# Routing attention followed by a mixture of experts: key masks on GpSimd, a first pair in halves, and three moved steps

## The chip, the cores and the metric

The kernel runs on one core of a Trainium2 chip. The metric is the device time of one execution in microseconds (us). A core has five engines that each work through a queue of their own, in order: TensorE multiplies matrices (its weight loads are shown apart), VectorE and ScalarE work on tensors element by element, GpSimd does so too and issues the indirect transfers, and SyncE issues most of the other transfers. Semaphores join them.

## The reference

Four batches, eight heads, 768 tokens, 64 values per head, and 16 cluster centroids per head. A query sees a key only where both have the same nearest centroid. The attention's output, 3072 rows of 512, then goes through a mixture of eight experts, of which each row takes one.

```
# q, k, v: 4 x 8 x 768 x 64; centroids: 8 x 16 x 64
q_assign = argmax(einsum("bhsd,hcd->bhsc", q_n, c_n), -1)   # q_n, k_n, c_n: normalised
k_assign = argmax(einsum("bhsd,hcd->bhsc", k_n, c_n), -1)
mask = q_assign[:, :, :, None] == k_assign[:, :, None, :]
attn = softmax(where(mask, q @ k.T / sqrt(64), -1e9))       # denominator + 1e-9
x = (attn @ v), laid out as 3072 x 512
logits = x @ w_gate                                         # 8 experts
e = argmax(logits); gate = softmax(logits)[e]
y = gate * (relu(x @ w1[e]) @ w2[e])                        # w1: 8 x 512 x 1024, w2: 8 x 1024 x 512
```

## The kernel before

*Attention.* The work is cut into 16 pairs: one batch and two heads, which share the 128 partitions (64 values each). Each pair goes through two halves of its 384 queries (`HS`) and six blocks of 128 keys. A slot is one block of one half, slots 0 to 11. In a slot `score` (L384) emits two f32 matmuls K x Q into a PSUM bank pair `sps` (three of them), two bf16 matmuls of 32 rows of a key mask and a query mask on top of that (`score_half`, L373 to L382, the matmuls at L379), and an exponential on ScalarE (L392) that writes one of twelve tiles `A`. The key mask `mk` and the query mask `mq` come from the one-hot cluster numbers, the key mask scaled by 2^60 and shifted, so that the exponential of a pair of different clusters is zero. `add_up` (L394) adds the tiles up on VectorE, one addition per slot from block 1 on. When all twelve slots are through, `attend` (L400) multiplies the tiles with V, half by half, and ScalarE copies each result to `oT`; slot 12 is between the two halves, slot 13 behind them. `sum_up` (L416) sums the accumulated tiles over the partitions on TensorE, in slot 2 of the next pair, and computes the pair's share of the gate's logits; `weights_of` (L433) takes the reciprocals, `rows` and `store` (slot 4) bring the output to DRAM.

*Preparing a pair.* `prepare(n, step)` (L469) has six steps. Step 0, `turn` (L274), is two VectorE transposes of q and k. Step 1, `similar` (L308), is four matmuls with the centroids. Step 2 (`assign0`, `assign1`, L322 to L334) and step 3 (`assign2`, L336) are seven VectorE instructions from the similarities to the transposed one-hots `ohT` (L348). Step 4, `place(n, 1)`, writes the key mask with four VectorE instructions (L361), and step 5, `place(n, 0)`, the query mask with four ScalarE copies (L359). Step 0 of pair n + 2 stands behind slot 12 of pair n (L837); steps 1 to 5 of pair n + 1 stand in slots 2, 5, 7, 8 and 11 of pair n (in pair 0, step 1 in slot 4), at L779.

*The first pair.* Its q and k come as two transfers each (L184), one of SyncE and one of ScalarE, in pieces of 256 bytes; twelve TensorE transposes (L267) and four copies (`first_turn`, L279) turn them, and the five steps for pair 0 follow one after the other (L819). The values of pair 0, the loads of pair 1 and the centroids' way to DRAM and back are issued in between.

*Gating.* While pairs 4 to 6, 8 to 10 and 12 to 13 run, the rows of the batch before are gated: `gate`, `gate_sum`, `choose`, `count` and `number` (L542), whose last act is six indirect transfers of GpSimd (L554) that scatter each row's record to its expert's list. `number` stands in slot 6 of pairs 6 and 10 and slot 3 of pair 13.

*Mixture of experts.* Ten turns, each one expert with a fixed number of rows (288, 288, 256, 288, 288, 384, 416, 416, 448, 128). `gather` (L685) fetches rows with indirect transfers, `weigh` (L702) scales them, `turn_rows` (L727) transposes them. `layer1` (L895) computes relu(x w1) with Strassen's scheme in Winograd's form: seven products instead of eight (L916), from sums of rows (`x_sums`), sums of weights (`w1_sums`, L756; all sums at L736) and additions of results (`add`, L874). It goes through two column halves; each half has seven places called hooks, 0 to 6 and 7 to 13, where other work may be put. In a half the hooks 4 and 5 of the seven come right behind the two additions. `h_sums` (L973) and `layer2` (L999) do the same for the second layer, with hooks of their own, and `write` (L991) scatters the rows. The dictionaries `h1` and `h2` say what stands at which hook of layers 1 and 2. The next turn's weight sums are given by `when` (L1158 to L1163); in turn 1 the sums 2 and 1 stand at hooks 9 and 10 of layer 1. In turn 3, `ask` (L622, hook 5) tests on VectorE that all softmax sums lie in a safe range, and `answer` (L632, hook 9) adds up the verdicts; a program that finds them outside runs a slower path at the end.

*The order of work.* Each engine's queue is the order in which the code emits instructions; nothing reorders them. The tile library adds the semaphores. So the hooks and slots decide what stands in front of what.

```
            for u, step in ((2 if n else 4, 1), (5, 2), (7, 3), (8, 4), (11, 5)):
                at_pair(n, u, prepare, n + 1, step)
...
            at_pair(n + 2 - last, 3 if last else 6, number, b)
...
                elif s == 1:
                    when = ((h1, 9), (h1, 10), (h2, 2), (h2, 3), (h2, 6), (h2, 6))
```

## Time and profile before

| | |
|---|---|
| median of three runs | 671.11 us (671.42, 668.75, 671.11) |
| the profiled execution | 672.25 us, of which the span of the profile is 670.7 |
| mean granted clock of TensorE | 0.992 |
| ScalarE | 300.0 us busy, 45% of the span |
| additions of `A` on VectorE, L398 | 160 of them, 0.945 to 0.948 us each |
| exponentials, L392 | 192, 0.811 us each |
| score matmuls, L379, f32 | 768, 159.3 us busy |
| first product of the experts' turns (L916) | starts at 337.1 us of the span |

The profile is one execution. Its first part gives each engine's busy time and share of the span; the second cuts the span into forty slices of 16.8 us, with a digit for the tenths of a slice in which an engine was busy. Groups of instructions are named by line, engine and operation, with the output on the left of the arrow. A row of a timeline shows the start, the duration of a run of like instructions, and in brackets the idle time ahead of them and what ended it. A row of TensorE's waits shows what waits, for what, and then the sum of the idle time, the number of waits and the longest. Durations of several instructions in one row run from the first's start to the last's end.

### The profile page before, as it was taken

Reading aid. Unit: us, or ns where it says so; the run is one execution under the profiler, and the core shown is the slowest. Engines: PE = TensorE matmul, PEld = TensorE weight load, DVE = VectorE, ACT = ScalarE, POOL = GpSimd, SP = SyncE. Lnnn points to the kernel's source line nnn. Section 1 sums busy time; section 2 is a strip of 40 time slices with the busy share of each in tenths; the row PEclk is TensorE's granted clock in tenths of the full one; section 3 lists DMA queues with packets and bytes.
Section 4 is the critical chain, followed back from the end, with each engine's and each line's share of the span. In section 5 each row is a group of like instructions: output and inputs, shape, how many; then the busy total and the mean of one; then the engine's idle time right before and its main releaser. Section 6 shows DMA issues by size and latency. Waiting matters only on the chain.

```text
span 670.7 us, 11366 instructions
## 1 busy us (share of the span) xinstructions
PE 649.9 (97%) x4210; PEld 425.7 (63%) x4210; DVE 512.3 (76%) x901; ACT 300.0 (45%) x522; POOL 127.3 (19%) x156
## 2 busy tenths in 40 slices
PE   5999999999999999999999999999999999999995
PEld 2444444454444455444575879989798887969773
DVE  5889999999999999999886868878778366572300
ACT  3666556657556565556622333243332331423210
POOL 4100000012000300033104704225240422130010
PEclk9899999999999999999999989999999999999998
DMA  6843455433455443347475586685675844625010
GB/s 118 191 86 72 82 95 95 66 73 72 77 95 95 65 81 73 70 115 239 115 266 142 189 297 217 253 321 156 275 239 229 261 160 138 221 93 182 8 48 18
DMA packets 191806, 95.36 MB, mean 142 GB/s; under 512 B 155967, under 2 KB 173887, under 8 KB 190464
## 3 DMA queue, kind: packets, MB, share of 16 engines
q1 hardware_dynamic: 184560, 81.15, 44.0%
q0 software_dynamic: 4928, 12.97, 5.8%
q8 instruction: 35, 0.57, 0.4%
q10 hardware_dynamic: 2256, 0.44, 0.4%
q14 instruction: 27, 0.22, 0.1%
HBM read 74.10 MB, written 20.70 MB: 141 GB/s over the span
## 4 chain that ended last, share of the span: by engine, by line
PE 77%; issue 9%; DVE 7%; POOL 2%; DMA 2%; ACT 1%; POOLq 0%; SPq 0%; DVEq 0%; ACTq 0%
PE sps L379 20%; PE mps L404 15%; PE bank L916 9%; PE sbank L916 7%; PE bank L1017 7%; PE bank L1036 7%; PE sbank L1017 5%; PE mps L427 2%; PE mps L312 2%; DMA xg<-x_rows,gi 1%; PE bank L885 1%; DVE acc L398 1%; DVE v L736 1%; DVE xT L727 1%; POOL tokens_of L554 1%
## 5 line engine op out<-in xcount | busy, mean ns | idle before, releaser
L392 ACT ACTIVATE A<-sps 128x768 f32<-128x768 f32 x192 | 153.5, 811 | 44.9 <-PE sps L379 44.1
L379 PE MATMUL sps<-qT,kT 64*128 64x384 f32 x768 | 159.3, 494 | 0.6 <-ACT A L392 0.6
L398 DVE TENSOR_TENSOR acc<-acc,A 128x768 f32<-128x768 f32 x128 | 121.4, 948 | 10.1 <-ACT A L392 2.8
L404 PE MATMUL mps<-A,v_in 128*64 128x384 f32 x768 | 127.4, 488 | 0.0
L379 PEld LDWEIGHTS sps<-qT,kT 64*128 64x128 f32 x768 | 67.1, 188 | 55.0 <-issue 51.4
L404 PEld LDWEIGHTS mps<-A,v_in 128*64 128x64 f32 x768 | 53.8, 137 | 70.5 <-issue 61.7
L991 POOL DMA_INDIRECT out_dram<-z,si x30 | 47.6, 1587 | 198.4 <-DVE z L874 169.3
L554 POOL DMA_INDIRECT tokens_of<-tg,pos_i x24 | 26.7, 1111 | 281.9 <-DVE pos_i L552 148.2
L379 PE MATMUL sps<-mq,mk 64*128 64x384 bf16 x384 | 63.5, 325 | 2.6 <-DVE mk L361 2.6
L1036 PE MATMUL bank<-w,h 128*128 128x512 f32 (+2 forms) x224 | 64.4, 596 | 0.0
L685 POOL DMA_INDIRECT xg<-x_rows,gi x30 | 42.7, 1423 | 48.2 <-DVE si L676 18.1
L359 ACT COPY mq<-ohT 32x384 bf16<-32x384 bf16 x62 | 31.6, 510 | 42.7 <-DVE ohT L348 41.8
L916 PE MATMUL sbank<-xc,a 128*128 128x144 f32 (+4 forms) x288 | 48.0, 310 | 0.2
L916 PE MATMUL bank<-xT,w 128*128 128x144 f32 (+4 forms) x288 | 47.8, 309 | 0.0
L874 DVE TENSOR_TENSOR h<-sbank,p 128x288 f32<-128x288 f32 (+4 forms) x18 | 9.2, 512 | 48.3 <-PE sbank L916 48.3
L916 PEld LDWEIGHTS bank<-xT,w 128*128 128x128 f32 x288 | 43.8, 191 | 2.6 <-issue 2.2
L1036 PEld LDWEIGHTS bank<-w,h 128*128 128x128 f32 (+2 forms) x224 | 24.7, 152 | 32.5 <-issue 32.3
L916 PEld LDWEIGHTS sbank<-xc,a 128*128 128x128 f32 x288 | 43.3, 191 | 0.9 <-ACT sbank L940 0.6
L379 PEld LDWEIGHTS <-mk 64*128 64x128 bf16 x384 | 19.5, 95 | 28.0 <-DVE mk L361 3.4
L934 ACT ACTIVATE h<-h 128x288 f32<-128x288 f32 (+4 forms) x36 | 17.6, 488 | 42.7 <-DVE h L874 42.5
L702 DVE TENSOR_TENSOR xw<-xg,sf 128x256 f32<-128x256 f32 (+2 forms) x60 | 32.8, 606 | 1.8 <-DMA xg<-x_rows,gi 1.6
L398 DVE TENSOR_TENSOR acc<-A 128x768 f32<-128x768 f32 x32 | 30.2, 945 | 3.1 <-ACT A L392 2.9
(208 smaller groups left out, 890.7 us busy)
## 6 DMA issues: line engine op xcount, KB each, us to landing
w<-in_moe_w_dram SPq DMA_DIRECT2D x20, 2048.0 KB, 12.0
v_in<-in_v_dram SPq DMA_DIRECT2D x32, 192.0 KB, 2.8
x_rows<-x SPq DMA_DIRECT2D x64, 96.0 KB, 2.4
turn_rows<-xw SPq DMA_DIRECT2D x23, 256.0 KB, 2.0
q_in<-in_q_dram SPq DMA_DIRECT2D x60, 96.0 KB, 3.2
k_in<-in_k_dram SPq DMA_DIRECT2D x60, 96.0 KB, 3.2
xs<-turn_rows SPq DMA_DIRECT2D x16, 144.0 KB, 2.8
xs<-turn_rows SPq DMA_DIRECT2D x8, 208.0 KB, 4.2
```

The source lines that it names most:

```text
L359: (nc.gpsimd.tensor_copy if n == 0 and h else nc.scalar.copy)(dst, src)
L379: nc.tensor.matmul(SP[n, h, j][:, a, 0:HS], lhsT=kt[rows, j * P : (j + 1) * P], rhs=qt[rows, h * HS : (h + 1) * HS], start=first, stop=not ...
L392: nc.scalar.activation(A[n, h, j], ps[:, :, 0:HS], AF.Exp, scale=D**-0.5)
L398: nc.vector.tensor_tensor(ACC[n, h], first, A[n, h, j], op=ALU.add)
L404: nc.tensor.matmul(O[n, h][D * a : D * (a + 1), 0:HS], lhsT=VIN[n][:, a, j, :], rhs=A[n, h, j][:, a, :], start=(j == 0), stop=(j == NQ - 1),)
L554: ins = nc.gpsimd.indirect_dma_start(out=t_d[:, :], out_offset=bass.IndirectOffsetOnAxis(ap=pos_i[:, i : i + 1], axis=0), in_=tg[:, b, i, ...
L685: nc.gpsimd.indirect_dma_start(out=xg[0:m], out_offset=None, in_=x_d[0:rows_in, :], in_offset=bass.IndirectOffsetOnAxis(ap=g["gi"][0:m, j ...
L702: nc.vector.tensor_tensor(xw[0:m, :, :, d2 * a : d2 * (a + 1)], xg[0:m].rearrange("p (r a d b) -> p a r b d", r=HP, a=2, b=DB)[:, a], g["s ...
L916: nc.tensor.matmul(ps[:, f * T2 : (f + 1) * T2], lhsT=w[:, k, (2 * j + f) * P : (2 * j + f + 1) * P], rhs=x[:, k, :], start=first and f + ...
L991: ins = nc.gpsimd.indirect_dma_start(out=out[:, :], out_offset=bass.IndirectOffsetOnAxis(ap=GR[s]["si"][0:rows, j : j + 1], axis=0), in_=z ...
L1017: nc.tensor.matmul(ps[:, 0:H], lhsT=x[:, k, :], rhs=y[:, k, :], start=first and k == 0, stop=k == 3, skip_group_check=not first,)
L1036: nc.tensor.matmul(ps[i * m : (i + 1) * m, :], lhsT=h[:, f, j * P : j * P + m], rhs=w[:, f, :], start=(k == 0), stop=(k == FB // n - 1),)
```

## The change

The change has six parts.

1. Pair 0. q and k come in one transfer each, both on SyncE, in pieces of 1536 bytes; the values of pair 0 and the loads of pair 1 stand right behind them, and the gate's weights move from ScalarE's queue to SyncE's. A new function `start_first` takes the place of the transposes, of `first_turn` and of the five steps: q and k are turned by matmuls with the identity, half by half, and copied by ScalarE; the similarities, the seven VectorE steps and the masks are done for each half of queries and keys, and the scores of blocks 0 to 2 stand in between. `assign0` to `assign2` get a `part` argument for that. The centroids' transfer to DRAM comes last.
2. The key masks of pairs 1 to 15 are written by GpSimd instead of VectorE. In pair 0 they stay with VectorE, while six of the eight query mask copies go to GpSimd.
3. In pair 0 the steps 1 to 4 for pair 1 stand in slots 6, 7, 8 and 9.
4. Step 0 of pair n + 2 stands in slot 10 of pair n instead of behind slot 12: ahead of the addition of the pair's last block.
5. In turn 1 the first two weight sums of turn 2 move from hooks 9 and 10 of layer 1 to its hook 12 and to hook 0 of layer 2.
6. In turn 3 `ask` and `answer` move from hooks 5 and 9 of layer 1 to its hook 12 and to hook 4 of layer 2.

One instruction of the centroids' norm is fused with its neighbour.

```diff
--- before.py
+++ after.py
@@ -178,9 +178,10 @@
             for d, src, name in ((QIN, q, "q_in"), (KIN, k, "k_in")):
                 t = d[n] = ld.tile([P, NI, Q4], F32, name=name)
                 if n == 0:
-                    t = d[n] = t.rearrange("p i d -> p (i d)").rearrange("p (j a d) -> p j a d", a=2, d=D)
-                    for a in range(2):
-                        (nc.sync, nc.scalar)[a].dma_start(out=t[:, :, a, :], in_=src[0, a].rearrange("(p j) d -> p j d", j=NQ))
+
+                    t = t.rearrange("p i d -> p (i d)").rearrange("p (a e) -> p a e", a=2)
+                    nc.sync.dma_start(out=t, in_=src[0, 0:2].rearrange("a (p j) d -> p a (j d)", j=NQ))
+                    d[n] = t.rearrange("p a (j d) -> p a j d", d=D)
                     continue
                 for r in range(4):
                     s = src[b, 2 * hp + r // 2, :, Q4 * (r % 2) : Q4 * (r % 2 + 1)]
@@ -202,6 +203,8 @@
         cin = consts.tile([P, D], F32)
         nc.scalar.dma_start(out=cin, in_=centroids.rearrange("h c d -> (h c) d"))
         load(0)
+        load_v(0)
+        load(1)
 
         csq = consts.tile([P, D], F32)
         cs2 = consts.tile([P, 1], F32)
@@ -221,7 +224,7 @@
         wgt = consts.tile([P, HP, Q4], F32)
         nc.gpsimd.memset(wgt, 0.0)
         for a in range(2):
-            nc.scalar.dma_start(
+            nc.sync.dma_start(
                 out=wgt[D * a : D * (a + 1), :, E * a : E * (a + 1)],
                 in_=moe_w_gate.rearrange("(h a d) e -> a d h e", a=2, d=D)[a],
             )
@@ -257,18 +259,6 @@
             cn, cin[:, None, :].to_broadcast([P, 2, D]), scalar1=cinv[:, 0:1], scalar2=None, op0=ALU.mult
         )
 
-        first = []
-        cps = ps_m.tile([P, 512], F32, name="mps")
-        for d in (QIN, KIN):
-            ps = ps_s.tile([P, 2, 512], F32, name="sps")
-            t = d.pop(0)
-            for j in range(NQ):
-                c0 = P * (j % 3)
-                nc.tensor.transpose(ps[:, j // 3, c0 : c0 + P], t[:, j].rearrange("p a d -> p (a d)"), ident)
-            first.append(ps)
-            if d is QIN:
-                nc.tensor.transpose(cps[:, 0:P], cn.rearrange("p a d -> p (a d)"), ident)
-
         QT, KT, SIM, OH = {}, {}, {}, {}
 
         def turn(n, w):
@@ -276,27 +266,6 @@
             dst[n] = qkt.tile([P, S], F32, name=name)
             nc.vector.transpose(dst[n], src.pop(n).rearrange("p i d -> p (i d)"))
 
-        def first_turn(w):
-            t = (QT, KT)[w][0] = qkt.tile([P, S], F32, name=("qT", "kT")[w])
-            for ins in (
-                nc.vector.tensor_copy(t[:, 0:HS], first[w][:, 0, 0:HS]), nc.scalar.copy(t[:, HS:S], first[w][:, 1, 0:HS])
-            ):
-                ins = getattr(ins, "ins", ins)
-                tc.declare_no_dep(ins, group=f"first_turn{w}", reason="disjoint columns")
-                tc.add_to_no_dep_group(f"first_turn{w}", ins)
-
-        first_turn(0)
-        cv = cps[:, 0:P].rearrange("p (h a c) -> p h a c", a=2, c=C)
-        for a in range(2):
-            nc.vector.tensor_copy(cT[D * a : D * (a + 1), :, a, :], cv[D * a : D * (a + 1), :, a, :])
-        for a in range(2):
-            nc.sync.dma_start(
-                out=cn_d.rearrange("(h a) d c -> a d h c", a=2)[a], in_=cT[D * a : D * (a + 1), :, a, :]
-            )
-
-        load_v(0)
-        load(1)
-        first_turn(1)
         first_cb = consts.tile([P, C], BF16)
         nc.gpsimd.tensor_copy(first_cb, first_c)
         ksc2 = consts.tile([P, 2], F32)
@@ -317,34 +286,34 @@
                 )
             SIM[n] = ps
 
-        G = 2 * HI
-
-        def assign0(n):
-
-            sim = asg.tile([P, HI, 2 * C], F32, name="sim")
-            nc.vector.transpose(sim.rearrange("p i c -> p (i c)"), SIM.pop(n)[:, 0:HS])
+        def assign0(n, part=1):
+
+            sim = asg.tile([P, HI, 2 * C], F32, name="sim")[:, 0 : HI // part]
+            nc.vector.transpose(sim.rearrange("p i c -> p (i c)"), SIM.pop(n)[:, 0 : HS // part])
             SIM[n] = sim.rearrange("p i (a c) -> p (i a) c", c=C)
 
...
@@ -355,15 +324,89 @@
                     dst = m[D * a : D * a + Q4, HS * h : HS * (h + 1)]
                     src = t[Q4 * g : Q4 * (g + 1), :]
                     if w == 0:
-
-                        (nc.gpsimd.tensor_copy if n == 0 and h else nc.scalar.copy)(dst, src)
+                        nc.scalar.copy(dst, src)
                     else:
-                        nc.vector.tensor_scalar(
+                        nc.gpsimd.tensor_scalar(
                             dst, src, scalar1=ksc2[Q4 * g : Q4 * (g + 1), a : a + 1],
                             scalar2=kscn2[Q4 * g : Q4 * (g + 1), a : a + 1], op0=ALU.mult, op1=ALU.add,
                         )
             if w == 0:
                 OH.pop(n)
+
+
+        def start_first():
+            HQ = HS // 2
+            cps = ps_m.tile([P, 512], F32, name="mps")
+            ps = [ps_s.tile([P, 2, 512], F32, name="sps") for _ in range(2)]
+            src = [d.pop(0) for d in (QIN, KIN)]
+            dst = [qkt.tile([P, S], F32, name=name) for name in ("qT", "kT")]
+            QT[0], KT[0] = dst
+
+            def turned(w, h):
+                for j in range(NQ // 2):
+                    for a in range(2):
+                        nc.tensor.matmul(
+                            ps[w][D * a : D * (a + 1), h, P * j : P * (j + 1)], lhsT=src[w][:, a, NQ // 2 * h + j, :], rhs=ident,
+                            start=True, stop=True,
+                        )
+
+            def copied(w, h):
+                nc.scalar.copy(dst[w][:, HS * h : HS * (h + 1)], ps[w][:, h, 0:HS])
+
+            def similar_half(h):
+                sps = SIM[0] = ps_m.tile([P, 512], F32, name="mps")
+                for g in range(4):
+                    c0 = HS * h + HQ * (g % 2)
+                    nc.tensor.matmul(
+                        sps[Q4 * g : Q4 * (g + 1), 0:HQ], lhsT=cT[:, 0].rearrange("p a c -> p (a c)"),
+                        rhs=dst[g // 2][:, c0 : c0 + HQ], start=True, stop=True,
+                    )
+
+            def place_half(h, w):
+                for g in (2 * w, 2 * w + 1):
+                    for a in range(2):
+                        c0 = HS * h + HQ * (g % 2)
+                        to = (MQ, MK)[w][0][D * a : D * a + Q4, c0 : c0 + HQ]
+                        rows = slice(Q4 * g, Q4 * (g + 1))
+                        if w == 0:
+                            (nc.gpsimd.tensor_copy if h or g else nc.scalar.copy)(to, OH[0][rows])
+                        else:
+                            nc.vector.tensor_scalar(
+                                to, OH[0][rows], scalar1=ksc2[rows, a : a + 1], scalar2=kscn2[rows, a : a + 1],
+                                op0=ALU.mult, op1=ALU.add,
+                            )
+
+            def clusters(h):
+                assign0(0, 2)
+                assign1(0, 2)
+                assign2(0, 2)
+                place_half(h, 1)
+                place_half(h, 0)
+
+            turned(0, 0)
+            copied(0, 0)
+            turned(1, 0)
+            copied(1, 0)
+            nc.tensor.transpose(cps[:, 0:P], cn.rearrange("p a d -> p (a d)"), ident)
+            cv = cps[:, 0:P].rearrange("p (h a c) -> p h a c", a=2, c=C)
+            for a in range(2):
+                nc.vector.tensor_copy(cT[D * a : D * (a + 1), :, a, :], cv[D * a : D * (a + 1), :, a, :])
+            turned(0, 1)
+            copied(0, 1)
+            similar_half(0)
+            turned(1, 1)
+            copied(1, 1)
+            clusters(0)
+            score_half(0, 0, 0, True)
+            similar_half(1)
+            for j in (1, 2):
+                score_half(0, 0, j, True)
+            clusters(1)
+            OH.pop(0)
+            for a in range(2):
+                nc.sync.dma_start(
+                    out=cn_d.rearrange("(h a) d c -> a d h c", a=2)[a], in_=cT[D * a : D * (a + 1), :, a, :]
+                )
 
 
         A, ACC, O, OT, SL = {}, {}, {}, {}, {}
@@ -383,9 +426,8 @@
 
         def score(n, h, j):
 
-            ahead = range(3) if n + h + j == 0 else (j,) if n + h or j > 2 else ()
-            for i in ahead:
-                score_half(n, h, i, True)
+            if n + h or j > 2:
+                score_half(n, h, j, True)
             score_half(n, h, j, False)
             ps = SP.pop((n, h, j))
             A[n, h, j] = ap.tile([P, 2, HS], F32, name="A")
@@ -776,8 +818,10 @@
                 at_pair(n, 2, sum_up, n - 1)
                 at_pair(n, 4, rows, n - 1)
                 at_pair(n, 4, store, n - 1)
-            for u, step in ((2 if n else 4, 1), (5, 2), (7, 3), (8, 4), (11, 5)):
+            for u, step in ((2 if n else 6, 1), (5 if n else 7, 2), (7 if n else 8, 3), (8 if n else 9, 4), (11, 5)):
                 at_pair(n, u, prepare, n + 1, step)
+
+            at_pair(n, 10, prepare, n + 2, 0)
         for b in range(B - 1):
             n = HP * (b + 1)
             last = b == B - 2
@@ -816,8 +860,7 @@
             for f in AT.pop((n, u), ()):
                 f()
 
-        for step in range(1, 6):
-            prepare(0, step)
+        start_first()
         routing_constants()
         prepare(1, 0)
         for n in range(NPAIR):
@@ -834,7 +877,6 @@
                     attend(n, h, j)
                 if h == 0:
                     between(n, 12)
-                    prepare(n + 2, 0)
             between(n, 13)
         assert not AT
 
@@ -1137,8 +1179,8 @@
                 at(h2, 7, indices, 2)
                 at(h2, 7, gather, 2)
             if s == 3:
-                at(h1, 5, ask)
-                at(h1, 9, answer)
+                at(h1, 12, ask)
+                at(h2, 4, answer)
             if s < last:
                 if 2 < s + 2 <= last:
                     places(s + 2)
@@ -1158,7 +1200,7 @@
                 if s == 0:
                     when = ((h2, 1), (h2, 2), (h2, 4), (h2, 5), (h2, 7), (h2, 7))
                 elif s == 1:
-                    when = ((h1, 9), (h1, 10), (h2, 2), (h2, 3), (h2, 6), (h2, 6))
+                    when = ((h1, 12), (h2, 0), (h2, 2), (h2, 3), (h2, 6), (h2, 6))
                 else:
                     when = ((h1, 9), (h1, 10), (h2, 1), (h2, 2), (h2, 2), (h2, 5))
                 if GR[s + 1]["T"] >= 2 * P:
```

More of the change, by code (lines that the diff above doesn't have):

```diff
@@ L250 @@
         nc.vector.reciprocal(cinv, cinv)
-        nc.vector.tensor_tensor(cinv, cinv, cs2, op=ALU.mult)
-        nc.vector.tensor_tensor(cinv, cinv, cnrm, op=ALU.add)
+        nc.vector.tensor_scalar(cinv, cinv, scalar1=cs2[:, 0:1], scalar2=cnrm[:, 0:1], op0=ALU.mult, op1=ALU.add)
         nc.vector.tensor_scalar(cinv, cinv, scalar1=0.5, scalar2=1e-6, op0=ALU.mult, op1=ALU.add)
@@ L318, in similar, with assign1, assign2 @@
             SIM[n] = ps
-        G = 2 * HI
-        def assign0(n):
-            sim = asg.tile([P, HI, 2 * C], F32, name="sim")
-            nc.vector.transpose(sim.rearrange("p i c -> p (i c)"), SIM.pop(n)[:, 0:HS])
+        def assign0(n, part=1):
+            sim = asg.tile([P, HI, 2 * C], F32, name="sim")[:, 0 : HI // part]
+            nc.vector.transpose(sim.rearrange("p i c -> p (i c)"), SIM.pop(n)[:, 0 : HS // part])
             SIM[n] = sim.rearrange("p i (a c) -> p (i a) c", c=C)
-        def assign1(n):
+        def assign1(n, part=1):
+            G = 2 * HI // part
             sim = SIM[n]
-            mx = asg.tile([P, G], F32, name="mx")
+            mx = asg.tile([P, 2 * HI], F32, name="mx")[:, 0:G]
             nc.vector.tensor_reduce(mx, sim, axis=AX, op=ALU.max)
-            ge = asg.tile([P, G, C], BF16, name="ge")
+            ge = asg.tile([P, 2 * HI, C], BF16, name="ge")[:, 0:G]
             nc.vector.tensor_tensor(ge, sim, mx.unsqueeze(2).to_broadcast([P, G, C]), op=ALU.is_ge)
             SIM[n] = ge
-        def assign2(n):
+        def assign2(n, part=1):
+            G = 2 * HI // part
             ge = SIM.pop(n)
-            rank = asg.tile([P, G, C], BF16, name="rank")
+            rank = asg.tile([P, 2 * HI, C], BF16, name="rank")[:, 0:G]
             nc.vector.tensor_tensor(rank, ge, first_cb[:, None, :].to_broadcast([P, G, C]), op=ALU.mult)
-            top = asg.tile([P, G], BF16, name="top")
+            top = asg.tile([P, 2 * HI], BF16, name="top")[:, 0:G]
             nc.vector.tensor_reduce(top, rank, axis=AX, op=ALU.max)
-            oh = asg.tile([P, HI, 2 * C], BF16, name="oh")
+            oh = asg.tile([P, HI, 2 * C], BF16, name="oh")[:, 0 : HI // part]
             nc.vector.tensor_tensor(
@@ L346, in assign2 @@
             )
-            OH[n] = asg.tile([P, HS], BF16, name="ohT")
+            OH[n] = asg.tile([P, HS], BF16, name="ohT")[:, 0 : HS // part]
             nc.vector.transpose(OH[n], oh.rearrange("p i c -> p (i c)"))
```

## The prediction

> **What bounds the kernel now.** I read the page first (busy times, forty slices), then TensorE's waits, then timelines around them.
>
> ```profile
> PE 649.9 (97%) x4210; PEld 425.7 (63%) x4210; DVE 512.3 (76%) x901; ACT 300.0 (45%) x522; POOL 127.3 (19%) x156
> PE   5999999999999999999999999999999999999995
> DVE  5889999999999999999886868878778366572300
> ...
> PE sps L267 <- POOL first_cb L301: 5.2, 1, 5.2
> PE sbank L916 <- DVE h L874: 3.4, 3, 2.4
> PE sps L379 <- DVE mk L361: 2.6, 2, 2.4
> PE mps L427 <- DVE acc L398: 0.9, 2, 0.7
> ```
>
> TensorE is the bound. Outside the first slice it idles in a dozen places; an edit pays only in one of these, and costs only where it opens a new one. VectorE is at nine tenths in the attention, so it is next in line there. "POOL first_cb" as releaser of the first transposes is an inference: GpSimd's identity is done at 2.26, and the q load issued by ScalarE at 1.24 lands 3.9 us later (the DMA view), at 5.1.
>
> In turn 1 VectorE queues two weight sums of turn 2 ahead of an addition TensorE waits for:
>
> ```profile
> 384.97 1.23 DVE L736 TENSOR_TENSOR a<-w,a 128x1024 f32<-128x1024 f32 x1
> 386.11 0.45 DVE L874 TENSOR_TENSOR h<-sbank,p 128x288 f32<-128x288 f32 x1
> 386.62 2.27 PE L916 MATMUL sbank<-xT,a 128*128 128x144 f32 x8 [2.42 <-DVE h L874]
> ```
>
> GpSimd and VectorE where pair 6 ends and pair 7 begins:
>
> ```profile
> 148.16 1.66 POOL L554 DMA_INDIRECT tokens_of<-tg,pos_i  x1 [127.64 <-DMA x_rows<-x]
> ...
> 155.49 0.97 POOL L554 DMA_INDIRECT tokens_of<-tg,pos_i  x1 [0.30 <-issue]
> ...
> 151.65 1.70 DVE L361 TENSOR_SCALAR mk<-ohT,ksc,kscn 32x384 bf16<-32x384 bf16 x4
> ...
> 155.41 0.33 PE L379 MATMUL sps<-mq,mk 64*128 64x384 bf16 x2
> ```
>
> GpSimd is occupied from 148.16 to 156.46 by six scatters; TensorE takes the first key mask at 155.41. Today that mask comes from VectorE at 151.65 and nobody notices.
>
> **What the Trainium skill says.** "TensorE: Matmul & The Clock Gate", Part 1: the clock is gated in free-running windows of about 3.4 us, and falls to half after an idle one. The trace agrees: the stretch 383.27 to 386.68, with 0.99 us of matmul, is followed by 3.40 us at a granted clock of 0.50; 14.63 to 18.04, with 1.82 us, likewise. "SBUF — State Buffer", Who interferes with whom: VectorE and GpSimd share a port pair as an exclusive lock; VectorE needs it in two-port modes, and with two SBUF inputs against a GpSimd instruction that reads SBUF. The trace agrees for the first half: the four mask instructions take 2.03 us beside two GpSimd copies (at 14.81), 1.58 alone (270.73). For additions it decides nothing. "GPSIMD Engine Reference", Engine selection: one-input elementwise work is about line rate; the row POOL COPY mq 32x384, 494 ns, agrees.
>
> **The change, part by part.** All in the profiled execution's time: span 670.7, 672.25 with what lies around it; the median of the three runs, 671.11, is 1.14 lower.
>
> *First pair in halves.* q and k come as one load each on SP, in pieces of 1536 bytes. A v load of 192 KB in such pieces lands after 2.8 us (median); twice the bytes should add about 0.5, so q lands at 0.8 + 3.3 = 4.1 instead of 5.1, k an estimated 1.0 later. ScalarE, rid of two issues, starts its table loads at 1.2 instead of 2.60, so it is free at 4.9 for the copies. Turning q half (1.3, by the 1.52 for today's six cold transposes, which the halves split into twice as many narrow matmuls), k half (1.3), centroids (0.3), second q half (1.3, part of it perhaps at full clock), half similarities (0.5): VectorE gets its first half at about 8.8; today the whole at 10.67. Its seven steps take 10.67 to 14.70 now, 4.03; at half length each keeps its fixed part (transpose 376 ns for 192 columns, 573 for 384), 2.7. Four half mask instructions beside GpSimd copies: 1.3. Second half 2.7, and 0.65 until the masks for block 3 are there: 8.8 + 2.7 + 1.3 + 2.7 + 0.65 = 16.2. Exp 3 then starts at 16.5; today (from 16.35, three at 0.82 on) at 18.8. The last seven exps run from 22.52 today, after the similarity of pair 1 held TensorE to 21.45 at half clock; that step now stands two blocks later. If a half-clock window falls in here again (TensorE idles 2 us before block 3) the first pair ends 1.7 earlier, if not 3.5. VectorE then has ten additions, pair 1's masks and pair 2's turn before the sums of pair 0, which caps the gain near 3. Taken: -2.4 (-0.8 to -3.5). The v load, pair 1's loads and the gate weights move in SP's queue; in exchange pair 1's k no longer comes late (VectorE waits 0.6 for it at 17.85 today). First use of these is pair 1's turn, near 17; they are issued by 9, so nothing, and at most 0.6 if other traffic holds them up.
>
> *Key masks to GpSimd, pairs 1 to 15.* VectorE loses 4 x 384 ns, 1.6 per pair with gaps. GpSimd's price: COPY 494 plus what the two-scalar form adds on 32x2 (233 against 180): 550 each; ends 500 and 850. In most pairs the one-hots are ready five us before the masks are due (49.9 and 55.7), so that is hidden. Not in pairs 7 and 11: the order of GpSimd's queue puts `number`'s six scatters in front of the masks. The scatters can't start earlier: pair 6's addition of block 3 waits for its exp (ends 141.29) and VectorE runs without a break from there to `pos_i`, with no mask in that stretch to lose. So 156.46 + 0.3 + 2 x 0.55 = 157.9 against 155.4: 2.5 of TensorE idle. Pair 11: scatters end at 236.55, mask due at 235.45: 2.5. Together +5.0 (4.7 to 6.3). A stall of 2.5 is as long as the one at 384.20, so it may bring a half-clock window; that costs half of 3.41, 1.7. I take one of two: +1.7 (0 to 3.4). In pair 14 the scatters (292.7) end before the one-hots (293.9).
>
> *Turn of pair n+2 ahead of the last addition.* VectorE's two transposes, 1.87, now stand in front of the addition that the sums wait for; the masks' 1.6 are gone; the lock adds c: GpSimd's four instructions can each hold up an addition by up to 0.55, so 0 to 2.2. I take 0.8, since the transposes leave room for some. The last addition comes 0.3 + c = 1.1 later. Today the slack before L427 is 2.0 in light pairs (55.5 against 57.5): hidden. In the pairs with gating it is about 0.4 (pair 5: 136.18 against 136.5; pair 9 alike): +0.7 each. In pairs 12 and 13 TensorE waits already (the 0.9 above): +1.05 each. Sum +3.4 (0.6 to 7).
>
> *End of attention.* Pairs 14 and 15 lose 1.6 of VectorE work with no later turn, so the waits at 341.30, 345.77 and 349.39 (0.17, 0.41, 0.20) close: -0.7 (0 to -0.8).
>
> *Turn 2's first sums.* Two of 1.22 leave the place before the addition. VectorE is then free at 383.70, adds to 384.15, TensorE goes on at 384.2: -2.4 idle, and the half-clock window at 386.69 goes (8 matmuls took 2.06 from start to next start, 0.98 elsewhere, and L1017 2.52 against 1.82: -1.8). One sum lands behind the last addition of the layer, ahead of the h sums, where a product and a single small tile cover it (h sums are needed at 388.9, there at 387.4). The other lands in layer 2, ahead of turn_rows, where VectorE is already just in time: `z<-sbank,p` ends at 401.92, its matmul starts at 401.98. Shifted, TensorE wants it at 397.5, and VectorE has it at 399.0: +1.4. Net -2.9 (-1.3 to -3.3).
>
> *Question on the sums, turn 3.* About 2 us of VectorE work leave the place before the addition; the 0.55 wait at 441.58 closes. `ask`, 1.05, then stands between the last addition and the h sums, covered as in turn 1; `answer`, 0.9, stands behind z's first half, where the next layer's addition has 0.9 to spare. -0.5.
>
> Sum: -2.4 + 5.0 + 1.7 + 3.4 - 0.7 - 2.9 - 0.5 = +3.6: 675.9 for the profiled execution, **674.7** as median.
>
> **Rivals.** *Masks not held up in the queue (not slower).* One mechanism, in pairs 7 and 11: if the six scatters leave GpSimd by 154 instead of 156.5, the masks of block 0 are there at 155.4, and the 5.0 and the 1.7 vanish: 672.25 + 3.6 - 6.7 = 669.2, as median 668.0; with additions that the lock spares, too, 665.2. It decides from 2.5 us earlier on. For it: VectorE loses 1.6 per pair, which could start the scatters sooner. Against it: the exp at 141.29 holds that chain wherever VectorE stands, and all three groups show six records of about 1 us with 0.3 between. *No lock on additions.* c = 0, sums +0.6: 2.8 less, 671.9. For it: no row of the trace shows an addition held up, and the transposes stand where the masks would meet additions. It decides below c of about 0.3. *Full lock.* c = 1.5 puts 1.4 on pairs 5 and 9, 1.8 on 12 and 13 and 0.2 on pair 4, 6.6 in all, and both stalls bring a half clock, 3.4: -6.5 (all gains) + 5.0 + 3.4 + 6.6 = +8.5, 679.6. For it: the 2.03 against 1.58 of the first masks.
>
> **How the numbers follow.** Forecast 42% (its own range 671.5 to 678.5), masks in time 18%, no lock 25%, full lock 15%. A measurement of this kernel can tell about 0.5% (3.4 us) from no change. Faster by more: 0.14 of the first rival and 0.05 of the second with a start at its upper end, 0.19. Within: 0.04 of the first, 0.18 of the second and the forecast's lower part, 0.12: 0.34. Slower: the rest, 0.47. The range 667 to 681 leaves out most of the first rival's lower half and the third's upper third.
>
> **What would show it.** Right: a wait of TensorE for GpSimd's mk of about 2.5, twice, at pairs 7 and 11; waits at L427's successor in pairs 6, 10, 13 and 14; no 2.4 in turn 1, but one of about 1.4 for z in its layer 2; first similarity on VectorE near 8.8 and exp 3 near 16.5. Wrong: masks in time in pairs 7 and 11, or additions that stretch in every pair.

## The result and the profile after

The changed kernel takes 683.27 us as median of six runs (680.07 to 685.13), the kernel before 671.14 (668.75 to 672.47): 1.0167 times as long, with an interval of 1.0138 to 1.0196. It is slower, by more than the forecast, and beyond the upper end of the range. Its profiled execution took 684.34, with a span of 682.6: 11.9 more than before. On the way to it the pages of both kernels look almost alike. The first sign is in the busy times: TensorE was busy 653.1 us instead of 649.9 with the same multiplications but for the start's few, and GpSimd 193.7 instead of 127.3.

```profile
PE 653.1 (96%) x4254; PEld 428.0 (63%) x4254; DVE 498.0 (73%) x849; ACT 300.3 (44%) x524; POOL 193.7 (28%) x220
```

TensorE's waits in the changed kernel (sum, number, longest, in us):

```profile
PE sps L422 <- POOL mk L329: 8.4, 4, 4.1
PE sps L348 <- DMA q_in<-in_q_dram: 4.5, 1, 4.5
PE mps L469 <- DVE acc L440: 2.8, 5, 1.0
PE sps L422 <- DVE mk L374: 1.8, 1, 1.8
PE sbank L1059 <- DVE z L916: 1.8, 3, 1.2
PE bank L958 <- DVE xc L778: 1.6, 1, 1.6
```

The wait of 2.4 in turn 1 is gone, one of 1.2 for z has come, and 8.4 us for GpSimd's masks stand on top. They are in pairs 7 and 11, as forecast, but longer. GpSimd, then TensorE, where pair 7 begins:

```profile
155.81 1.01 POOL L596 DMA_INDIRECT tokens_of<-tg,pos_i  x1 [0.30 <-issue]
158.18 2.16 POOL L329 TENSOR_SCALAR mk<-ohT,ksc,kscn 32x384 bf16<-32x384 bf16 x3 [1.35 <-DMA tokens_of<-tg,pos_i]
```

```profile
154.24 0.92 PE L422 MATMUL sps<-qT,kT 64*128 64x384 f32 x4
158.89 0.50 PE L422 MATMUL sps<-mq,mk 64*128 64x384 bf16 x1 [3.73 <-POOL mk L329]
159.64 0.50 PE L422 MATMUL sps<-mq,mk 64*128 64x384 bf16 x1 [0.25 <-POOL mk L329]
```

The last of the six scatters leaves GpSimd at 156.82. The first mask starts only at 158.18: GpSimd stands idle for 1.35 us, and what ends that is the landing of a scatter. In pair 11 the same gap is 2.56:

```profile
246.15 2.93 POOL L329 TENSOR_SCALAR mk<-ohT,ksc,kscn 32x384 bf16<-32x384 bf16 x4 [2.56 <-DMA tokens_of<-tg,pos_i]
```

And the time lost does not end with the wait. Five stretches around it, with TensorE's granted clock near the end of each line:

```profile
core 0: us, PE busy (x) PEld busy (x) DVE busy (x) ACT busy (x) POOL busy (x), PEclk, DMA share, GB/s
154.70:158.11 3.41, 0.45 (x4) 0.00 (x0) 1.27 (x2) 0.13 (x1) 1.82 (x2) 1.00 0.43 121
158.11:161.52 3.41, 2.38 (x9) 1.45 (x11) 0.00 (x0) 0.81 (x1) 2.64 (x4) 0.50 0.00 0
161.52:164.94 3.42, 3.42 (x32) 1.69 (x33) 1.62 (x2) 1.62 (x2) 0.00 (x0) 0.50 0.01 2
164.94:168.30 3.36, 3.36 (x34) 1.64 (x28) 2.06 (x7) 1.31 (x2) 0.00 (x0) 1.00 0.00 0
```

Two stretches at half clock follow, 6.83 us; behind pair 11's wait it is one, 3.41. At most half of these 10.2 us, 5.1, can be lost by that.

To see where time comes in, I laid the starts of the exponentials beside those of the kernel before, pair by pair. The attention's order is the same in all kernels here, so that a shift that stays constant over a pair says that nothing happened in it. The changed kernel is 0.76 ahead from pair 0 to pair 6, 0.40 ahead at the end of pair 6, 6.76 behind within pair 7, 13.40 behind within pair 11, and 13.43 behind when the attention ends. The experts' turns bring it to 11.9.

### The profile page after: what moved, and what is told of

It is laid out like the page before. It is cut to its first block, busy times and chain, and to the rows that moved or that the text cites. A ratio compares the mean times of both kernels' runs of the same rounds, so it can differ in the third digit from the quotient of the medians.

```text
span 682.6 us, 11510 instructions
## 1 busy us (share of the span) xinstructions
PE 653.1 (96%) x4254; PEld 428.0 (63%) x4254; DVE 498.0 (73%) x849; ACT 300.3 (44%) x524; POOL 193.7 (28%) x220
## 4 chain that ended last, share of the span: by engine, by line
PE 36%; DVE 12%; DMA 3%; issue 2%; SPq 1%; ACT 0%; POOL 0%; DVEq 0%; POOLq 0%
PE bank L958 9%; PE sbank L958 8%; PE bank L1078 7%; PE bank L1059 7%; PE sbank L1059 5%; DVE acc L440 2%; DVE a L778 2%; DVE xw L744 2%; DVE v L778 1%; DVE xT L769 1%; DMA turn_rows<-xw 1%; PE bank L927 1%; DMA xs<-turn_rows 1%; DMA sf<-tokens_of 1%; DVE z L916 1%
## 5 line engine op out<-in xcount | busy, mean ns | idle before, releaser
L422 PE MATMUL sps<-qT,kT 64*128 64x384 f32 x768 | 163.6, 503 | 0.0
L440 DVE TENSOR_TENSOR acc<-acc,A 128x768 f32<-128x768 f32 x128 | 127.5, 996 | 11.7 <-ACT A L434 5.5
L329 POOL TENSOR_SCALAR mk<-ohT,ksc,kscn 32x384 bf16<-32x384 bf16 x60 | 61.3, 1022 | 171.8 <-DVE ohT L317 156.2
L422 PEld LDWEIGHTS sps<-qT,kT 64*128 64x128 f32 x768 | 68.6, 190 | 52.1 <-issue 49.0
L422 PE MATMUL sps<-mq,mk 64*128 64x384 bf16 x384 | 67.4, 330 | 10.3 <-POOL mk L329 8.4
L422 PEld LDWEIGHTS <-mk 64*128 64x128 bf16 x384 | 21.0, 96 | 39.0 <-POOL mk L329 10.8
```

The lines of the kernel that those rows point to most:

```text
L329: nc.gpsimd.tensor_scalar(dst, src, scalar1=ksc2[Q4 * g : Q4 * (g + 1), a : a + 1], scalar2=kscn2[Q4 * g : Q4 * (g + 1), a : a + 1], op0=A ...
L422: nc.tensor.matmul(SP[n, h, j][:, a, 0:HS], lhsT=kt[rows, j * P : (j + 1) * P], rhs=qt[rows, h * HS : (h + 1) * HS], start=first, stop=not ...
L440: nc.vector.tensor_tensor(ACC[n, h], first, A[n, h, j], op=ALU.add)
```

## The experiments

The kernel before was measured again beside each group of runs (medians of 671.14 to 672.35), so two rows are compared by their ratios, not by their medians. The first column of numbers is the median of the run. The others are the shift of the exponentials against the kernel before at the start of four pairs, from the traces (+ is later, us).

| kernel | median | ratio to before, interval | pair 2 | pair 8 | pair 12 | pair 15 |
|---|---|---|---|---|---|---|
| changed | 683.27 | 1.0167, 1.0138 to 1.0196 | -0.76 | +6.76 | +13.40 | +13.43 |
| all masks on VectorE | 677.63 | 1.0084, 1.0052 to 1.0116 | -0.58 | +1.80 | +4.18 | +5.86 |
| masks of pairs 7, 11 on VectorE | 671.25 | 0.9989, 0.9973 to 1.0004 | -0.95 | +0.31 | +1.50 | +1.55 |
| scatters behind the masks | 669.08 | 0.9960, 0.9945 to 0.9976 | -1.43 | -1.12 | -0.84 | -0.80 |
| four scatters in front | 675.71 | 1.0066, 1.0042 to 1.0090 | -1.72 | +0.94 | +3.66 | +3.69 |
| waits filled, ten matmuls | 679.47 | 1.0102, 1.0064 to 1.0140 | -0.69 | +6.38 | +13.41 | +13.44 |
| waits filled, five matmuls | 677.14 | 1.0083, 1.0054 to 1.0112 | -0.79 | +4.17 | +9.57 | +9.60 |
| before, masks alone | 681.19 | 1.0129, 1.0104 to 1.0154 | +0.49 | +7.25 | +13.11 | +11.99 |
| before, masks, scatters behind | 667.88 | 0.9928, 0.9901 to 0.9954 | +0.08 | -0.36 | -0.83 | -1.93 |
| scatters and turn behind | 665.58 | 0.9907, 0.9870 to 0.9944 | -1.01 | -1.44 | -1.92 | -3.03 |
| the same, sums behind z | 664.99 | 0.9885, 0.9860 to 0.9911 | -0.54 | -0.97 | -1.44 | -2.55 |
| before, start alone | 671.63 | 0.9981, 0.9962 to 0.9999 | -0.77 | -0.78 | -0.79 | -0.80 |
| before, hooks alone | 669.21 | 0.9955, 0.9939 to 0.9971 | +0.53 | +0.52 | +0.52 | +0.51 |

Two theories stood at the beginning. Theory A: nearly all the loss is in pairs 7 and 11, from masks that stand behind the scatters. Theory B: GpSimd's masks and VectorE's additions hold each other up in all pairs. Three runs tell them apart.

**All masks back on VectorE.**

```diff
-                        nc.gpsimd.tensor_scalar(
+                        nc.vector.tensor_scalar(
```

> The changed kernel with the key masks of pairs 1 to 15 back on VectorE; nothing else undone. Theory A (all the loss is in pairs 7 and 11, where the first mask stands behind six scatters and waits for their landing, 7.2 + 6.3 us by the exponentials' starts): those 13.5 us go; in return VectorE has 1.6 us more per pair in front of the sums while the two transposes also stand there, so the waits for the last addition grow by about 1 us in each of pairs 5, 9, 12 and 13: 683.3 - 13.5 + 4 = about 674. Theory B (GpSimd's masks and VectorE's additions hold each other up all along, the masks at 1.02 us instead of 0.55): VectorE's additions fall back from 0.996 to 0.948 us, and the time falls below the kernel before's 671.

Measured: 677.63. The 13.5 us go, and 6.4 come back in the pairs with gating, more than the 4 of theory A, which had expected 674: TensorE waits seven times, 7.6 us in all, for the last addition.

```profile
PE mps L469 <- DVE acc L440: 7.6, 7, 2.2
```

It is not below the kernel before, as theory B wanted. But the lock is there. Additions beside VectorE's masks, beside GpSimd's masks, and GpSimd's masks themselves (the last from the changed kernel; count, then busy time and mean):

```profile
L440 DVE TENSOR_TENSOR acc<-acc,A 128x768 f32<-128x768 f32 x128 | 120.9, 945 | 9.3 <-ACT A L434 4.0
```

```profile
L440 DVE TENSOR_TENSOR acc<-acc,A 128x768 f32<-128x768 f32 x128 | 127.5, 996 | 11.7 <-ACT A L434 5.5
L329 POOL TENSOR_SCALAR mk<-ohT,ksc,kscn 32x384 bf16<-32x384 bf16 x60 | 61.3, 1022 | 171.8 <-DVE ohT L317 156.2
```

Taken one by one in the changed kernel's trace, the 40 additions that overlap a mask of GpSimd's take 1109 ns in the mean, the other 88 take 945.

**Masks of two pairs on VectorE.**

```diff
-                        nc.gpsimd.tensor_scalar(
+                        (nc.vector if n in (7, 11) else nc.gpsimd).tensor_scalar(
```

> The changed kernel with the key masks of pairs 7 and 11 alone on VectorE, all others still on GpSimd. Theory A: both stalls and the half clock behind them go, 683.3 - 13.5 = about 670. Theory B: only two of fifteen pairs are relieved, so most of the loss stays, above 680.

Measured: 671.25, with no wait for a mask outside pair 0. Relieving two of fifteen pairs brings the whole loss back, as theory A said; theory B had expected more than 680.

**Scatters behind the masks.** `number` keeps its arithmetic in slot 6, and a new function issues the six scatters in slot 9.

```diff
+            if not last:
+                at_pair(n + 2, 9, scatter, b)
```

> The changed kernel with all masks on GpSimd, but the six scatters of batches 0 and 1 issued in slot 9 of pairs 6 and 10, behind the next pair's masks; number's arithmetic stays in slot 6. Theory A: as with the masks of two pairs on VectorE, about 670, and no wait of TensorE for a key mask outside pair 0. Theory B: the masks are as slow as before, so above 680.

Measured: 669.08, 0.9960 of the kernel before. The masks are as slow as before (1078 ns in the mean), and no mask is waited for in pairs 1 to 15. TensorE's waits for additions of `A` and for masks in this kernel:

```profile
PE mps L469 <- DVE acc L440: 2.7, 4, 1.0
PE sps L422 <- DVE mk L374: 1.8, 1, 1.8
```

Theory B falls as the cause of the loss.

**Place in the queue, or landing?** Four of the six scatters stay in front (the edit against the run before).

```diff
-                at_pair(n + 2, 9, scatter, b)
+                at_pair(n + 2, 6, scatter, b, range(4))
+                at_pair(n + 2, 9, scatter, b, range(4, TC))
```

> The changed kernel with four of the six scatters of batches 0 and 1 in slot 6 as before, and the last two in slot 9, behind the masks. It tells the place in GpSimd's queue from the wait for landing: the fourth scatter leaves GpSimd at about 154.2 (pair 7) and 241.0 (pair 11) in the changed kernel's times, TensorE wants the first mask at 155.2 and 242.7, and a mask alone takes 0.73. If only the queue counts: the masks are there at 155.0 and 241.8, no wait, and the time of the kernel with all scatters behind, 669. If the first mask also waits until these four have landed, 1.35 to 2.56 behind the last one's end: waits of 1.2 to 2.4 and 0.4 to 1.6, and 671 to 675, with half a clock window at most.

Measured: TensorE waits 1.42 and 0.42 in pair 7, 1.51 and 0.42 in pair 11. GpSimd in pair 7:

```profile
151.59 1.69 POOL L604 DMA_INDIRECT tokens_of<-tg,pos_i  x1 [0.30 <-issue]
154.78 3.04 POOL L329 TENSOR_SCALAR mk<-ohT,ksc,kscn 32x384 bf16<-32x384 bf16 x4 [1.51 <-DMA tokens_of<-tg,pos_i]
```

The fourth scatter is out at 153.28, a little before TensorE is ready (154.19), and the mask still starts at 154.78. So both count: the queue by its length, and the landing by 1.5 and 1.7 us more. (A mask alone takes 0.65 to 0.67, not the 0.73 of the expectation.) The built programs say why the landing counts. The first mask behind indirect transfers is given a wait on their completion, though its data don't come from them. GpSimd's queue at pair 7 of the changed kernel (the first of the six scatters, which has waits of its own, is left out):

```
L596 DMACopy tokens_of<-tg,pos_i x5
L329 TensorScalarPtr mk<-ohT,ksc,kscn 32x384 [waits DMASW2, 3, 1, 4, 0, 5, DVE, PE]
L329 TensorScalarPtr mk<-ohT,ksc,kscn 32x384 [waits PE] x3
```

It is so for the first mask behind GpSimd's transfers in every kernel with masks there: in pairs 7, 11, 14 and 15 of the changed kernel, in 8, 12, 14 and 15 where the scatters stand behind the masks. Which rule of the tile library puts it there was not looked into. The median, 675.71, lies above the profiled execution (673.2); by the shifts, the two places cost the profiled one 4.7 us, of which the waits are 3.8. The other four executions ran at a mean granted clock of 0.990 to 0.994 for its 0.997, and a stretch of 3.41 us at half clock lowers that mean by 0.0025. So by estimate each of them had one to three such stretches more; no trace shows where.

**What follows the waits.** Matmuls that nobody reads fill them.

```diff
+            if n in (7, 11) and h + j == 0:
+                spare = ps_m.tile([P, 512], F32, name="mps")
+                for _ in range(10):
+                    nc.tensor.matmul(spare[:, 0:HS], lhsT=ident, rhs=QT[n][:, 0:HS], start=True, stop=True)
```

> The changed kernel with ten extra f32 matmuls of the identity and 384 columns of q (about 3.3 us by the 0.33 us that two such half-width matmuls take together) in front of the first mask matmul of pairs 7 and 11, into a spare PSUM tile that nobody reads. They fill most of the 3.7 and 4.1 us in which TensorE waits there. If the 5.1 us that come on top of the two waits are the half clock that follows an idle stretch: the waits stay, the 5.1 go, 683.3 - 5.1 = about 678. If they are something else (the exponentials queued up behind the mask, for one): 683 as before.

Measured: 679.47; the size was wrong. In the trace an f32 matmul of 384 columns is two instructions, 0.67 us in all. So the ten take 6.7 us, not 3.3, and outlast the waits:

```profile
155.14 6.72 PE L434 MATMUL mps<-qT,ident 128*128 128x384 f32 x20
161.79 0.34 PE L422 MATMUL sps<-mq,mk 64*128 64x384 bf16 x2
```

So they lose themselves what the wait and the half clock lost before, and the attention ends 13.44 late. So the lower time is not won in the attention: the rest of the kernel, which is the same code, takes 6.1 us less than before in this trace and 1.5 less in the changed kernel's (see *End of attention* below). One thing can be read from it: no half clock follows, and pair 7 is 6.43 late at its first exponential and 6.38 at its fourth, where the changed kernel went from 4.37 to 6.76. With five of them:

```diff
-                for _ in range(10):
+                for _ in range(5):
```

> The changed kernel with five extra matmuls instead of ten in front of the first mask matmul of pairs 7 and 11: 0.67 us each by the run with ten, so 3.4, which is less than the waits of 3.7 and 4.1. If the loss beyond the waits is the half clock: no half-clock window there, the exponentials of pair 7 lose 4.0 and those of pair 11 4.4, and nothing behind that, 5.1 below the changed kernel, about 679. If not: 684.

Measured: 677.14. No half clock at either place, and all four executions ran at a mean granted clock of 0.994 to 0.997, the changed kernel's six at 0.986 to 0.992. The attention ends 9.60 late instead of 13.43, 3.8 less, where 5.1 was expected. That the median came near the expected 679 is luck: here too the rest of the kernel takes 5.5 us less than before, not 1.5. Nothing is lost behind the first exponential of pair 7 or 11, and the loss up to it is that of the changed kernel (4.7 and 5.1 us for 4.8 and 5.2). That the half clock is a loss of its own, caused by the idle stretch and not by the masks, is shown, with 3.8 us for both places. The other 1.3 of the 5.1 stays with the waits. A part of it is that block 0's two mask matmuls, elsewhere side by side, come one after the other, 0.33 more in each pair:

```profile
158.84 0.33 PE L422 MATMUL sps<-mq,mk 64*128 64x384 bf16 x1 [0.30 <-POOL mk L329]
159.59 0.33 PE L422 MATMUL sps<-mq,mk 64*128 64x384 bf16 x1 [0.42 <-POOL mk L329]
```

**Part 2 alone on the kernel before.**

```diff
-                        nc.vector.tensor_scalar(
+                        (nc.gpsimd if n else nc.vector).tensor_scalar(
```

> The kernel before with part 2 alone: the key masks of pairs 1 to 15 on GpSimd. Theory A: both stalls with their half clock, +13.5, less what VectorE wins in the pairs with gating, 2.0 by the exponentials of the run with the turn behind slot 12: 672.3 + 11.5 = about 684. Theory B (the turn ahead of the last addition makes the loss, masks alone are harmless): below 675.

Measured: 681.19. TensorE's waits are nearly those of the changed kernel, and so are three stretches of half clock behind them and the shifts:

```profile
PE sps L379 <- POOL mk L361: 8.1, 4, 3.8
```

This one edit slows the kernel by nearly as much as the whole change (1.0129 for 1.0167).

**Part 2 alone, with the scatters behind the masks** (the last edit and that of the run with the scatters behind, on the kernel before).

> The kernel before with part 2 and the scatters of batches 0 and 1 behind the next pair's masks; nothing else of the change. Theory A: no stall, and the 2.0 us that VectorE wins: about 670.3. Rival: VectorE's 1.6 us per pair lie beside TensorE's work anyway, and the time is that of the kernel before, 672.3.

Measured: 667.88. The profiled execution took 670.68, close to the 670.3 of theory A; what the three others gained beyond it no trace shows. In it the attention gains 0.42 and 0.43 in pairs 6 and 10, 0.36 and 0.75 in pairs 13 and 14: 2.0, in four places, and nothing anywhere else. The 0.75 is the wait for the last addition. In pairs 6 and 10 the kernel before shows no wait. There the similarities of kT, which run side by side with those of qT where both are ready, had to follow them, because `turn` had written kT only at 137.94. TensorE's rows in pair 6, first before, then here (runs of like instructions; the eight take 1.36 us in the first, 0.94 in the second):

```profile
137.47 0.81 PE L312 MATMUL mps<-qT,cT 128*32 128x384 f32 x4
137.99 0.84 PE L312 MATMUL mps<-kT,cT 128*32 128x384 f32 x4
```

```profile
137.54 0.49 PE L312 MATMUL mps<-qT,cT 128*32 128x384 f32 x2
137.65 0.52 PE L312 MATMUL mps<-kT,cT 128*32 128x384 f32 x2
137.87 0.49 PE L312 MATMUL mps<-qT,cT 128*32 128x384 f32 x2
137.99 0.49 PE L312 MATMUL mps<-kT,cT 128*32 128x384 f32 x2
```

VectorE was late there, and it counted as TensorE's own work.

**The turn behind slot 12.** The kernel with the scatters behind the masks, and part 4 undone.

```diff
-            at_pair(n, 10, prepare, n + 2, 0)
...
                     between(n, 12)
+                    prepare(n + 2, 0)
```

> The kernel with the scatters behind the masks, and with the turn of pair n + 2 put back behind slot 12. Theory A: the waits of TensorE for the last addition (0.36, 0.36, 0.95 and 0.99 in pairs 5, 9, 12 and 13) come from the two transposes ahead of it, 1.87 us, of which the masks' 1.6 on GpSimd make good only a part; they vanish, and the pairs gain what the exponentials showed, 0.7 to 1.5 us: about 668. Theory B: the lock between GpSimd's masks and VectorE makes the additions late, wherever the turn stands: the waits stay, 669.

Measured: 665.58. No wait for an addition is left before the experts' turns, though GpSimd's masks are slower still (1194 ns). TensorE's longest waits in this kernel:

```profile
PE sps L348 <- POOL ksc L241: 4.4, 1, 4.4
PE sps L422 <- DVE mk L374: 1.8, 1, 1.8
PE sbank L1068 <- DVE z L925: 1.8, 3, 1.2
```

From pair 2 to pair 15 it gains 2.0 us against the kernel before (-1.01 to -3.03), where the one with the turn ahead lost 0.6 (-1.43 to -0.80). So the moved turn cost the change 2.6, about all that the moved masks are worth.

**Sums behind z.** In the same kernel:

```diff
-                    when = ((h1, 12), (h2, 0), (h2, 2), (h2, 3), (h2, 6), (h2, 6))
+                    when = ((h1, 12), (h2, 0), (h2, 5), (h2, 5), (h2, 6), (h2, 6))
```

> As the run with the turn behind slot 12, and in turn 1 the third and fourth weight sum of turn 2 behind both additions of z (hook 5 of layer 2 instead of 2 and 3). Theory: the wait of TensorE for z in turn 1's layer 2, 1.17 us, goes and nothing comes in its place: about 667, the fastest so far. Rival: turn 2's layer 1 then waits for these sums at its fifth or seventh product, and nothing is gained: 668.

Measured: 664.99, which can't be told from the run before it. The 1.17 for z is gone; turn 2's layer 1 waits 1.46 and 0.80 for additions, behind the work that was pushed back (the first of the two):

```profile
402.52 1.16 PE L967 MATMUL sbank<-xT,a 128*128 128x128 f32 x8 [1.46 <-DVE h L925]
```

The rival was right that nothing is gained, though the waits are for additions of `h` and not for the sums themselves. Still, this kernel and the one before it are the fastest of the study, at 0.9885 and 0.9907.

**The start alone** (parts 1 and 3 on the kernel before).

> The kernel before with parts 1 and 3 alone (the first pair in halves; pair 0's slots), all key masks but pair 0's on VectorE, turn and hooks as before. By the traces of the changed kernels, pair 1 starts 0.6 to 0.95 us earlier where a half-clock window follows the wait for the second half's masks (1.8 us), and 1.4 earlier where it doesn't: 670 to 671 against 671.5 for the kernel before. The prediction had -2.4: 669.

Measured: 671.63, and a shift of -0.77 that stays through the whole attention. That is what the start gives where a half clock follows the wait of 1.81. In the traces of two kernels above (scatters behind, four in front) none followed the same wait; they were ahead by 1.43 and 1.72.

**The hooks alone** (parts 5 and 6 on the kernel before).

> The kernel before with parts 5 and 6 alone (turn 2's first sums, and ask and answer in turn 3). Forecast of the prediction: -2.9 and -0.5, so 3.4 below the kernel before, at about 668: no wait of 2.4 in turn 1 and no half clock behind it, one of about 1.2 for z instead, no 0.55 in turn 3. Rival: the time is lost again further on, where VectorE gets the same work later, and less than 1 us remains.

Measured: 669.21, 0.9955: 3 us by the runs, 2.1 between the start and the end of the experts' turns in the trace. Turn 1 gains 4.0 and gives back 1.1 at z. Turn 3 gains 0.7 where `ask` stood, and loses 0.8 in its first half; turn 4 loses 0.6. The two losses are alike: a load of `sf` lands 1.2 and 0.8 us after VectorE is ready for it, the addition behind it comes later, and TensorE waits 0.68 and 0.57 for the ScalarE copy that follows. So the rival is right in part: what the move in turn 3 wins is lost again close by.

## Why the prediction was wrong

The forecast was right about the place and the direction, wrong about the size of two terms that belong together: they are 6.8 too small, of the 8.3 by which the sum missed. That the other errors (+1.6 at the start, -2.7 in the sums, about +2 outside the forecast, the rest small) nearly cancel is luck. Shifts and waits of the profiled executions, against the terms of its sum:

| step | forecast | measured |
|---|---|---|
| first pair in halves | -2.4 | -0.8 |
| waits for the masks in pairs 7 and 11 | +5.0 | +8.4 |
| half clock behind them | +1.7 | +5.1 (3.8 of it half clock by the run with five matmuls) |
| sums later (turn, lock) | +3.4 | +0.7 |
| end of attention | -0.7 | -0.3 |
| turn 1 | -2.9 | -3.0 |
| turn 3 | -0.5 | about -0.2 (-0.7, and +0.5 in turn 4 behind it) |
| not in the forecast: rows late at turn 1's start (+1.4), a wait in turn 3's first half for which the trace names nothing (+1.1), smaller ones | 0 | about +2 |
| sum | +3.6 | +11.9 |

*Masks behind the scatters.* The step that failed is "So 156.46 + 0.3 + 2 x 0.55 = 157.9 against 155.4". It took the time at which the last scatter leaves GpSimd for the time at which GpSimd is free. The 0.3 was 1.35 and 2.56, until the scatters had landed, and a mask that runs alone took 0.65, with 0.1 to the next, not 0.55. The landing stands in the answer on transfers of the kernel before (its last figure is the median time from issue to landing):

```profile
tokens_of<-tg,pos_i POOLq DMA_INDIRECT x24, 2.7
```

I didn't use it, because the masks' data have nothing to do with these transfers; the wait is in the program all the same, and could have been read there before the run. The upper end that I gave, 6.3, left it out as well.

*Half clock.* "I take one of two: +1.7" failed. Both waits brought one, and pair 7's lasted two stretches. It follows from the wait that was mis-sized at 2.5: the two waits of 3.7 and 4.1 in the changed kernel and the two of 3.7 and 3.8 in the run with part 2 alone all brought one, those of 1.4 and 1.5 in the trace with four scatters in front none. That the length decides is not shown: the wait of 1.81 in the start mostly brought one, and the forecast's "after an idle one" is too narrow, for in the kernel before it came after a stretch with 1.82 us of matmul.

*Sums.* The waits for the last addition grew in the four pairs named, from 0.9 to 2.8 us, so by 1.9 for the forecast's 3.4. Pairs 5 and 9 got 0.36 each for 0.7, pair 12 0.95 for 1.05, but pair 13 only 0.28 more. There the forecast had misread its line: the 0.9 is a wait of 0.71 in pair 13 and one of 0.17 at the end of the attention, and pair 12 had none. The lock, c, was 0.4 per pair, not 0.8, if it is estimated from the mean of the additions (8 times 0.05); what it cost the last addition is not shown apart. Additions that stretch in every pair were one of the forecast's signs of being wrong; three or four stretch in thirteen of the sixteen pairs, and it is not what made it wrong. And 1.2 was won back in the pairs that follow, where kT is now ready early and the similarities run side by side (in pair 14 the eight took 1.60 us before and take 1.12 now): a wait of before that no row of waits showed, so that the forecast missed it. The Trainium skill's page "SBUF — State Buffer", Who interferes with whom, lets VectorE with two SBUF inputs and a GpSimd instruction that reads SBUF shut each other out; the runs agree, with additions of 945 ns where no mask of GpSimd's overlaps and 1109 where one does, and it falls on GpSimd more than on VectorE: 0.65 for the shortest mask, 1.20 in the median, 2.09 for the longest.

*Start.* The first similarity reached VectorE at 9.19 (forecast 8.8), and TensorE took block 3's mask at 16.78 (16.2), for two sets of masks that took 1.5 and 1.6 instead of 1.3. The exponential behind it started at 17.53, for the forecast's 16.5, and in the kernel before at 18.45, not at the 18.8 that the forecast took. So 0.92 was won there instead of 2.3. Then a half clock came. For that case the forecast itself had 1.7, where 0.8 came; its -2.4 was taken between that and the 3 without one.

*End of attention.* VectorE had 1.6 less to do in the last pairs, and then stood waiting for rows that go through DRAM and back:

```profile
343.40 1.38 DVE L769 STREAM_TRANSPOSE xT<-xs 128x1152 f32<-128x1152 f32 x1 [3.09 <-DMA xs<-turn_rows]
```

Before, the same wait was 2.11; the gain went into a transfer. In the two kernels with filled waits it was 1.15 and 1.35, and the end of the attention and turn 0 gained 2.0. At turn 1's beginning VectorE waited 4.20 for the same trip in the changed kernel, for 2.82 before, and TensorE 1.59 behind it; so it was in four of the kernels above, while the others waited 2.55 to 2.98. Why the trip takes these lengths is open. TensorE is up to 3.3 us apart by it between kernels whose turns are the same code, so the shifts within the attention carry the argument here, and medians a few us apart do not.

*Turn 1* came as forecast, the wait for z (1.17 for 1.4) included.

## What to carry to other kernels

Before work moves to an engine, look at what that engine's queue holds at the moment the work is due, not at how busy it is: the same masks were worth -2.0 us or +11.5 in the attention, by six transfers that stood in front of them in two of fifteen pairs. A queue that issues transfers can hold up the next instruction until they have landed, as the programs here do, so read the waits in the built program. Waits of TensorE of 3.7 and 4.1 us cost here about half as much again in half clock (3.8 us for 8.4), so a stall that is put on its path must be priced with it.

## What the runs showed of the hardware beyond that

GpSimd's 32x384 masks took 0.65 to 0.67 us with VectorE at rest and 1.20 in the median beside it, yet the kernels with the slowest masks (1194 ns) were the fastest. The same wait of 1.81 us in the start was followed by a half clock of 3.41 in most kernels' traces and by none in two. The wait of 2.4 to 2.6 us in turn 1 brought one in the kernel before and in two other kernels with the old hooks, and none in the run with part 2 alone. In that run and in the one with the hooks alone the start, which is untouched there, had a half clock of 6.83 instead of 3.41, and pair 2 began 0.5 us later than in the kernel before.
